# Reordering the prologue of an mLSTM cell with a SwiGLU FFN: 64-row turns, a GpSimd gate, late maxima behind the first products

## Chip, cores and metric

One core of one Trainium2 chip. The metric is the device time of one execution in microseconds (us), as the median of several runs. A profile of one execution shows where the time goes.

## The reference

The work is an mLSTM cell whose output feeds a feed-forward block. The cell runs over 768 tokens for 4 batches of 8 heads with 40 features. Its gates are stabilized with a running maximum:

```
m_new  = max(f[t] + m, i[t])
C      = exp(f[t] + m - m_new) * C + exp(i[t] - m_new) * v[t] k[t]^T
n      = exp(f[t] + m - m_new) * n + exp(i[t] - m_new) * k[t]
y[t]   = sigmoid(o[t]) * (C q[t]) / max(|n q[t]|, 1)
```

The rows y (3072 tokens by 320) go through `(silu(x @ w_gate) * (x @ w_val)) @ w_out` with a hidden width of 1536. The inputs of the cell are float32. The three weights are float64 and are turned into float32 on the chip, word by word.

## The kernel before

**Stages.** The tokens of all four batches are worked on in six groups of 128. The attention part of group 0 is the prologue; after it, the FFN of group g runs on TensorE while the other engines and short stretches of TensorE prepare group g+1. The FFN has twelve hidden blocks `hidden(g, m)` (gate and value products, silu on ScalarE, product on VectorE) and then the projection.

**Order.** The schedule is written out by hand: on each engine, instructions run in the order of the program. The lists `slots` and `ahead` say which pieces of other work are put behind or into block m of group 0. `first=` work of a block stands ahead of that block's silu and product, work of `slots[m]` behind them.

**Prologue (functions `first_*`).** Batches are handled in two pairs P of two batches u (heads 16P to 16P+15). W0 holds the decay weights of group 0, made by `first_mask`, `first_inputs`, `first_maxima` on TensorE and `first_exp` on ScalarE. `first_turn` turns k and q into feature rows with transposes of 128 x 128; `turn_one` does the same with transposes of 64 token rows, as the later groups do. `first_scores(P)` makes k-q products and VectorE multiplies them into W0. `first_own(u)` multiplies W0 with v; `first_x(u)` divides; `first_gate(P)` multiplies with the sigmoid of the output gate (`sig`) and copies the first 64 columns behind the last ones (GpSimd). `first_seam(P)` turns the rows into the FFN's input xT; `first_state` and `first_kept` make the state for group 1. `burn(n)` issues n idle products of 512 columns on TensorE.

**Maxima of the later groups.** `late_sums` scans the forget gates (VectorE) and subtracts (GpSimd); `late_maxima` is two small copies and a scan over 640 columns on 32 partitions; `late_decay` makes the decays; their exponential, `decay_rows`, `late_turns` (turn g and e, 10 transposes) and `decay` follow in the slots. The maxima go out to `M_dram`, and `weights_load(1)` reads them back into w_sb.

**Weights.** `piece_load(p)` loads piece p: gate columns into partitions 0 to 63 on SyncE's queue, value columns into partitions 64 to 127 on ScalarE's queue for p below 5. Piece 0 is block 0, piece 1 block 1, piece 2 blocks 2 and 3, piece 3 blocks 4 and 5. A converted block takes `scale(j)` (two ScalarE operations, L190 and L192), `join(j)` (two VectorE operations, L199 and L200) and `rounded(j)` (L207, on VectorE or on GpSimd, whose default it is). `top` has one buffer, so scale(j+1) waits for join(j). The `raw` tile has two buffers; pieces 2, 3 and 4 are loaded into parts of h_sb and wo_sb that are not in use yet, and piece 2's part holds W0 of batches 0 to 2, so that load waits for `first_own(2)`.

**PSUM.** Tiles come from two rings of four banks, "cell" and "gen". The FFN's products take "gen".

Of the kernel before, what the change touches and what calls it, by code (L numbers as in the profile page):

```python
# [12 lines left out]
U32 = mybir.dt.uint32  # L13
AF = mybir.ActivationFunctionType
ALU = mybir.AluOpType
# [9 lines left out]
def kernel(  # L25
# [47 lines left out]
    def flat(t):  # L73
        return t.rearrange("p c t -> p (c t)")

    def bank(name, tag="cell"):
        return psum.tile([128, 512], F32, name=name, tag=tag)
# [41 lines left out]
    def copy(eng, dst, src):  # L119
        if eng is nc.scalar:  # L120
            nc.scalar.copy(dst, src)
        else:
            eng.tensor_copy(dst, src)
# [58 lines left out]
                for c in range(0, n, 2):  # L182
                    blocks[NFC + (m + c) // 2] = (lo[:, c:c + 2], hi[:, c:c + 2], wo_sb[:, m + c:m + c + 2, :])

    def scale(j):
        if j in blocks:
            lo, hi, dst = blocks[j]
            a, d = hi.shape[1], hi.shape[2]
            top = conv.tile([128, NKC * 128], F32, name="top", bufs=1).rearrange("p (a d) -> p a d", a=a)
            nc.scalar.mul(top, hi.bitcast(F32), 2.0 ** -112)  # L190
            low = conv.tile([128, NKC * 128], I32, name="low").rearrange("p (a d) -> p a d", a=a)
            nc.scalar.mul(low, lo, 2.0 ** -29)  # L192
            blocks[j] = (low, top.bitcast(U32), dst)

    def join(j):
        if j in blocks:
# [81 lines left out]
    def late_maxima():  # L278
        nc.vector.tensor_copy(step1[:, 0:1, 0:1], f0[0:BH, end].unsqueeze(1))
        nc.vector.tensor_copy(step1[:, 1:, 0:1], f_sb[:, 0:NL - 1, last])  # L280
        nc.vector.tensor_tensor_scan(flat(M_sb), flat(step1), flat(i_sb), M0[0:BH, end], op0=ALU.add, op1=ALU.max)
# [6 lines left out]
    M_dram = tc.dram_tile([BH, S - L], F32, name="M_dram")  # L288


    def turn_one(P, src, dst, engs):
        tp = [bank("tp_kq").rearrange("p (a t) -> p a t", t=SUB) for _ in range(2)]
        for a in range(UA):
            h = P * UH + 2 * a
            for i in range(2):
                nc.tensor.transpose(tp[i][:, a, :], src[half(i), h:h + 2, :].rearrange("p h d -> p (h d)"),  # L296
                                    ident[half(i), half(i)])
        for i in range(2):
            copy(engs[i], dst[:, P * UA:(P + 1) * UA, half(i)], tp[i])
# [128 lines left out]
    def xT(n):  # L428
        return xTs[max(n - 1, 0) % 2]
# [36 lines left out]
    def burn(n, tag="cell"):  # L466
        t = bank("burn", tag)
        for _ in range(n):
            nc.tensor.matmul(t, lhsT=junk[:, 0:128], rhs=junk, start=True, stop=True)  # L469
# [2 lines left out]
        return slice(u * BH, (u + 1) * BH)  # L472

    A, V, G = nc.scalar, nc.vector, nc.gpsimd
    HH = H // 2
    wps = {}

# [21 lines left out]
    def first_values(P):  # L499
        nc.gpsimd.tensor_copy(w_end[:, heads(P)], W0[:, heads(P), end])  # L500
        nc.gpsimd.tensor_tensor(vw_sb[:, heads(P)], v_sb[:, heads(P)], w_end[:, heads(P)].to_broadcast([128, UH, D1]),
                                op=ALU.mult)

    def first_turn(P, src, dst, engs):
        for b in range(2):
            tp = bank("tp_kq").rearrange("p (a t) -> p a t", t=L)
            for a in range(UA // 2):
                h = P * UH + b * H + 2 * a
                nc.tensor.transpose(tp[:, a, :], src[:, h:h + 2, :].rearrange("p h d -> p (h d)"), ident)  # L509
            a = P * UA + b * UA // 2  # L510
            copy(engs[b], dst[:, a:a + UA // 2, :], tp)

    def first_scores(P):
        for b in range(2):
            sp = [bank("sp").rearrange("p (a t) -> p a t", t=L) for _ in range(2)]
            a0 = P * UA + b * UA // 2
            for a in range(UA // 2):
                for two in range(2):
                    nc.tensor.matmul(sp[two][:, a, :], lhsT=kT[half(two), a0 + a, :], rhs=qT[half(two), a0 + a, :],  # L519
                                     start=True, stop=True)  # L520
            W = W0[:, 2 * a0:2 * a0 + H].rearrange("p (a two) t -> p two a t", two=2)
            for two in range(2):
                nc.vector.tensor_tensor(W[:, two], sp[two], W[:, two], op=ALU.mult)
# [3 lines left out]
    def first_own(u):  # L527
        first_y[u] = bank("first_y", "gen")[:, 0:H * D1].rearrange("p (h d) -> p h d", d=D1)
        for h in range(H):
            nc.tensor.matmul(first_y[u][:, h, :], lhsT=W0[:, u * H + h, :], rhs=v_sb[:, u * H + h, :], start=True, stop=True)  # L530
# [7 lines left out]
        nc.vector.tensor_tensor(x_sb[:, u, 0:DM].rearrange("p (h d) -> p h d", d=D), y[:, :, 0:D],  # L538
                                den.to_broadcast([128, H, D]), op=ALU.mult)

    def first_gate(P):
        for u in (2 * P, 2 * P + 1):
            x = x_sb[:, u, 0:DM].rearrange("p (h d) -> p h d", d=D)
            nc.vector.tensor_tensor(x, x, o_sb[:, u * H:(u + 1) * H], op=ALU.mult)
        nc.gpsimd.tensor_copy(x_sb[:, 2 * P:2 * P + 2, DM:], x_sb[:, 2 * P:2 * P + 2, 0:HP])

    def first_state(P, tag="cell"):
# [7 lines left out]
    def first_kept(P, ps, eng):  # L555
        copy(eng, state(2)[:, P * UA:(P + 1) * UA], ps)

    def first_seam(P, engs):
        for c, eng in zip(range(0, NKC, 2), engs):
            cs = range(c, min(c + 2, NKC))  # L560
            tp = bank("tp_x")[:, 0:len(cs) * 2 * L].rearrange("p (c u s) -> p c u s", u=2, s=L)
            for w in cs:
                for b in range(2):
                    nc.tensor.transpose(tp[:, w - c, b, :], x_sb[:, 2 * P + b, ds(PAIRS[w][0] * HP, 2 * HP)], ident)
            copy(eng, xT(0)[:, c:c + len(cs), 2 * P * L:(2 * P + 2) * L].rearrange("p c (u s) -> p c u s", u=2), tp)

    burn(7)
    banks = [(u, j) for j in range(2) for u in range(B)]
# [6 lines left out]
    first_exp(1)  # L575
    first_values(0)
    first_scores(0)
    first_own(0)
    late_sums()
    first_turn(1, k_sb, kT, (A, A))  # L580
    first_x(0)
    first_turn(1, q_sb, qT, (A, V))
    load(o_sb, o_gate, 0, 1)
    piece_load(0)
    piece_load(1)
    late_maxima()
    first_own(1)
    first_values(1)
    first_scores(1)
    first_x(1)  # L590
    sig(0)
    burn(3)
    first_own(2)
    piece_load(2, h_sb[:, 1:1 + NKC])
    sig(1)
    burn(2)
    first_own(3)
    first_gate(0)
    first_x(2)
    first_x(3)  # L600
    first_gate(1)
    first_seam(0, (A, A, V))
    scale(0)
    ps1 = first_state(1, "gen")
    burn(1, "gen")
    piece_load(3, h_sb[:, NH - NKC:])
    join(0)
    first_seam(1, (A, A, V))
    rounded(0, V)
    first_kept(0, first_state(0), A)  # L610
    first_kept(1, ps1, V)
    late_decay()
    convert(1, V)
    nc.scalar.activation(warm, warm, AF.Silu)
    piece_load(4, wo_sb)
    piece_load(5)
    nc.sync.dma_start(out=M_dram, in_=flat(M_sb))


    pair = early.tile([BH, PP], F32)  # L620
# [102 lines left out]
    def load_all(dst, a, n):  # L723
        for P in range(2):
            load(dst, a, n, P)

    run = lambda f, *a: (lambda: f(*a))


    on_vector = (9, 10, 11)  # L730
# [1 line left out]
    ahead[0] = []  # L732
    ahead.update({4: [6], 5: [7, 8], 6: [9], 7: [10], 8: [11], 9: [], 10: [], 11: []})
    slots = {
        0: [run(convert, 2, V), run(load_all, k_sb, k, 1), run(load_all, q_sb, q, 1)],
        1: [run(piece_load, 6), run(nc.scalar.activation, step1, step1, AF.Exp), run(decay_rows)],
        2: [run(late_turns), run(weights_load, 1), run(load_all, v_sb, v, 1)],
        3: [run(decay)],
        5: [run(turn, 0, (A, A), (A, V))],
        6: [run(turn, 1, (A, A), (A, V)), run(piece_load, 7)],  # L740
        7: [run(weights_sub, 1, 0), run(weights_mask, 0), run(weights_sub, 1, 1), run(weights_mask, 1), run(nc.gpsimd.memset, q_sb, 0.0)],
# [112 lines left out]
```

## Time and profile before

| | |
|---|---|
| median of 3 runs | 552.01 us (551.99 to 552.12) |
| the profiled execution | 551.91 us |
| its span, first to last instruction | 549.9 us |
| busy: TensorE, VectorE, ScalarE, GpSimd | 544.7, 235.7, 135.8, 104.1 us |
| first product of the FFN starts | 31.91 us |
| last product ends | 546.8 us |
| granted TensorE clock | 1.000 |

Times in the views count from the first instruction of the span. A chain row is start, duration, engine, tile written and line of the kernel. In a timeline row, the bracket tells how long the engine was idle before it and what ended the wait. TensorE matmul ends are modelled. A row of a waits view tells who waited for whom, the total, how often, and the longest. A row of a stretch gives its limits and length, then the busy time of TensorE, its weight loads, VectorE, ScalarE and GpSimd, the granted clock, the DMA share, and GB/s.

### The profile page before, as it was taken

How to read it: one execution, taken by the hardware profiler on the slowest of the kernel's cores; microseconds unless marked ns; L12 is line 12 of the kernel's file. 1: busy time of each engine (PE TensorE's matmuls, PEld its weight loads, DVE VectorE, ACT ScalarE, POOL GpSimd, SP SyncE). 2: the span in 40 equal slices, each digit the busy share in tenths (PEclk: the TensorE clock that was granted, in tenths of full speed). 3: DMA queues.
4: the chain of work that ended last, by engine and by line, in shares of the span. 5: the costliest groups of instructions: out<-in, count | busy, mean ns of one | idle time of the engine just before them, and what ended most of it. 6: DMA issues, size and time to landing. Idle time of an engine off the chain costs nothing.

```text
span 549.9 us, 11590 instructions
## 1 busy us (share of the span) xinstructions
PE 544.7 (99%) x4987; PEld 311.6 (57%) x4989; DVE 235.7 (43%) x397; ACT 135.8 (25%) x203; POOL 104.1 (19%) x95
## 2 busy tenths in 40 slices
PE   8999999999999999999999999999999999999997
PEld 4964556774555575545575545576455567444475
DVE  5985769971346232455421545431436621111100
ACT  3376755252110133011024101115110100111100
POOL 2304265673011060011142011114001100000000
PEclk9999999999999999999999999999999999999999
DMA  9999997997431862660654551395000231000000
GB/s 126 183 287 181 193 268 157 149 108 113 52 50 26 129 109 55 74 73 12 102 104 100 64 71 14 58 145 115 1 1 2 35 63 37 12 1 0 2 24 24
DMA packets 223994, 45.69 MB, mean 83 GB/s; under 512 B 214504, under 2 KB 219112, under 8 KB 223944
## 3 DMA queue, kind: packets, MB, share of 16 engines
q1 hardware_dynamic: 222036, 42.11, 47.3%
q10 hardware_dynamic: 1908, 2.85, 2.1%
q8 instruction: 39, 0.64, 0.5%
q14 instruction: 11, 0.09, 0.1%
HBM read 35.68 MB, written 4.01 MB: 72 GB/s over the span
## 4 chain that ended last, share of the span: by engine, by line
PE 98%; DVE 1%; ACT 0%; issue 0%; ACTq 0%; DVEq 0%
PE gv_ps L654 57%; PE o_ps L670 24%; PE o_ps L677 5%; PE inter L377 2%; PE sp L331 2%; PE intra L382 2%; PE add L353 1%; PE first_y L530 1%; PE burn L469 1%; PE tp_kq L509 1%; PE sp L519 1%; PE wps L480 0%; PE tp_kq L296 0%; PE wps L484 0%; PE wps L489 0%; PE tp_x L439 0%
## 5 line engine op out<-in xcount | busy, mean ns | idle before, releaser
L654 PE MATMUL gv_ps<-xT,wgv_sb 64*128 64x512 f32 x1440 | 316.5, 593 | 0.3 <-DVE wgv_sb L207 0.3
L654 PEld LDWEIGHTS gv_ps<-xT,wgv_sb 64*128 64x128 f32 x1440 | 137.9, 187 | 159.2 <-issue 157.3
L660 DVE TENSOR_TENSOR h_sb<-sg,gv_ps 128x512 f32<-128x512 f32 x72 | 49.5, 688 | 216.9 <-ACT sg L659 216.9
L670 PE MATMUL o_ps<-wo_sb,h_sb 128*128 128x320 f32 x480 | 130.5, 434 | 0.0
L670 PEld LDWEIGHTS o_ps<-wo_sb,h_sb 128*128 128x128 f32 x480 | 90.8, 190 | 40.9 <-issue 3.8
L659 ACT ACTIVATE sg<-gv_ps 128x512 f32<-128x512 f32 x72 | 43.0, 597 | 266.3 <-PE gv_ps L654 266.1
L456 POOL TENSOR_SCALAR_AFFINE_SELECT w_sb<-w_sb 64x1024 f32<-64x1024 f32 x20 | 28.4, 1422 | 62.5 <-DVE w_sb L451 61.5
L362 POOL TENSOR_TENSOR C<-C,dec 128x328 f32<-128x328 f32 x20 | 14.5, 736 | 135.7 <-DVE C L369 135.7
L664 ACT COPY z_sb<-o_ps 128x320 f32<-128x320 f32 x24 | 10.0, 422 | 94.1 <-PE o_ps L670 90.6
L403 POOL TENSOR_TENSOR o_sb<-o_sb,y_sb 128x640 f32<-128x640 f32 x10 | 14.2, 1426 | 79.1 <-DVE y_sb L394 79.1
L677 PE MATMUL o_ps<-wo_sb,h_sb 128*128 128x320 f32 x96 | 26.9, 437 | 0.0
L451 DVE TENSOR_TENSOR w_sb<-g_T,w_sb 128x1024 f32<-128x1024 f32 x10 | 13.1, 1356 | 27.7 <-DMA w_sb<-M_dram 27.7
L426 DVE STREAM_TRANSPOSE xT<-x_sq 128x640 f32<-128x640 f32 x16 | 12.5, 822 | 22.4 <-DMA x_sq<-x_sb 22.4
L677 PEld LDWEIGHTS o_ps<-wo_sb,h_sb 128*128 128x128 f32 x96 | 17.9, 190 | 7.2
L394 DVE TENSOR_TENSOR y_sb<-y_sb,intra 64x328 f32<-64x328 f32 x40 | 19.7, 492 | 0.7
L369 DVE TENSOR_TENSOR C<-C,add 40x328 f32<-40x328 f32 (+1 forms) x36 | 17.7, 493 | 1.2 <-POOL C L362 0.6
L377 PEld LDWEIGHTS inter<-C,qT 64*64 64x64 f32 x640 | 10.2, 134 | 7.3 <-issue 6.1
L207 POOL TENSOR_TENSOR wgv_sb<-wgv_sb,low 128x640 int32<-128x640 int32 x6 | 9.2, 1539 | 24.0 <-DVE wgv_sb L200 24.0
L460 ACT ACTIVATE w_sb<-w_sb 128x1024 f32<-128x1024 f32 x10 | 10.6, 1058 | 11.8 <-POOL w_sb L456 11.7
L341 POOL TENSOR_TENSOR vw_sb<-v_sb,w_sb 128x656 f32<-128x656 f32 x10 | 12.8, 1303 | 0.4
L338 DVE TENSOR_TENSOR w_sb<-sp,w_sb 128x512 f32<-128x512 f32 x20 | 12.7, 682 | 0.0
L397 DVE TENSOR_SCALAR den<-den 128x16 f32<-128x16 f32 x10 | 12.1, 1214 | 0.3
(132 smaller groups left out, 345.3 us busy)
## 6 DMA issues: line engine op xcount, KB each, us to landing
w_sb<-M_dram SPq DMA_DIRECT2D x10, 512.0 KB, 8.7
x_sq<-x_sb SPq DMA_DIRECT2D x128, 40.0 KB, 2.0
k_sb<-in_k_dram SPq DMA_DIRECT2D x12, 320.0 KB, 6.0
v_sb<-in_v_dram SPq DMA_DIRECT2D x12, 320.0 KB, 5.8
o_sb<-in_o_gate_dram SPq DMA_DIRECT2D x12, 320.0 KB, 5.4
raw<-in_moe_w_out_dram SPq DMA_DIRECT2D x3, 1280.0 KB, 8.2
out_dram<-z_sb SPq DMA_DIRECT2D x24, 160.0 KB, 1.8
q_sb<-in_q_dram SPq DMA_DIRECT2D x32, 64.0 KB, 2.3
```

The lines of the kernel that those rows point to most:

```text
L362: nc.gpsimd.tensor_tensor(state(s + 1)[:, a], state(s)[:, a], dec[:, s - 2, a].unsqueeze(2).to_broadcast([128, UA, D1]), op=ALU.mult)
L369: nc.vector.tensor_tensor(c, c, ps[r], op=ALU.add)
L377: nc.tensor.matmul(inter[two][half(i), a, :], lhsT=qT[half(two), P * UA + a, half(i)], rhs=state(2 * n + i)[half(two), P * UA + a, :], sta ...
L394: nc.vector.tensor_tensor(t, t, intra[i][half(c)], op=ALU.add)
L403: eng.tensor_tensor(o, o, y[:, :, 0:D], op=ALU.mult)
L451: nc.vector.tensor_tensor(w_sb[:, heads(P)], gb, w_sb[:, heads(P)], op=ALU.subtract)
L456: nc.gpsimd.affine_select(w, w, compare_op=ALU.is_ge, fill=NEG, base=0, pattern=[[0, UH], [1, SUB]], channel_multiplier=-1)
L654: nc.tensor.matmul(ps[i], lhsT=wgv_sb[half(i), m, PAIRS[kc][i] if g < 2 else kc, :], rhs=x[half(i), kc, :], start=(kc == 0), stop=(kc == N ...
L659: nc.scalar.activation(sg, ps[0], AF.Silu)
L660: nc.vector.tensor_tensor(hid(g, m), sg, ps[1], op=ALU.mult)
L670: nc.tensor.matmul(p, lhsT=hid(g, m)[:, ts(u, L)], rhs=wo_sb[:, m, :], start=(m == 0), stop=(m == NFC - 1))
L677: nc.tensor.matmul(ps[u], lhsT=hid(g, m)[:, ts(u, L)], rhs=wo_sb[:, m, :], start=(m == 0), stop=(m == NFC - 1))
```

## The change

In the prologue, k and q of pair 1 are turned with `turn_one` (64-row transposes), k's into "gen" banks and ahead of `first_own(0)`. `first_gate(0)` runs on GpSimd. `first_x(1)` stands ahead of `first_scores(1)`; piece 1 is loaded behind `sig(0)`; three of the burns are gone. `scale` is split, and its first half stands between the first and the second copy of `first_seam(0)`; `rounded(0)` stands ahead of `first_seam(1)`. `late_maxima` moves into slot 0 of group 0, `late_decay` into slot 1, the store to `M_dram` behind the first k loads in slot 0; the exponential and `decay_rows` move to slot 2, `late_turns` to slot 3, `decay` to slot 4.

```diff
-    def scale(j):
+    def scale_top(j):
         if j in blocks:
             lo, hi, dst = blocks[j]
...
             nc.scalar.mul(top, hi.bitcast(F32), 2.0 ** -112)
+            blocks[j] = (lo, top.bitcast(U32), dst)
+
+    def scale_low(j):
+        if j in blocks:
+            lo, top, dst = blocks[j]
...
             nc.scalar.mul(low, lo, 2.0 ** -29)
-            blocks[j] = (low, top.bitcast(U32), dst)
+            blocks[j] = (low, top, dst)
+
+    def scale(j):
+        scale_top(j)
+        scale_low(j)
...
-    def turn_one(P, src, dst, engs):
-        tp = [bank("tp_kq").rearrange("p (a t) -> p a t", t=SUB) for _ in range(2)]
+    def turn_one(P, src, dst, engs, tag="cell"):
+        tp = [bank("tp_kq", tag).rearrange("p (a t) -> p a t", t=SUB) for _ in range(2)]
...
-    def first_gate(P):
+    def first_gate(P, eng):
...
-            nc.vector.tensor_tensor(x, x, o_sb[:, u * H:(u + 1) * H], op=ALU.mult)
+            eng.tensor_tensor(x, x, o_sb[:, u * H:(u + 1) * H], op=ALU.mult)
...
-    def first_seam(P, engs):
+    def first_seam(P, engs, between=None):
...
             copy(eng, xT(0)[:, c:c + len(cs), 2 * P * L:(2 * P + 2) * L].rearrange("p c (u s) -> p c u s", u=2), tp)
+            if between and c == 0:
+                between()
...
     first_scores(0)
+    turn_one(1, k_sb, kT, (A, A), "gen")
     first_own(0)
     late_sums()
-    first_turn(1, k_sb, kT, (A, A))
+    turn_one(1, q_sb, qT, (A, V))
     first_x(0)
-    first_turn(1, q_sb, qT, (A, V))
     load(o_sb, o_gate, 0, 1)
     piece_load(0)
-    piece_load(1)
-    late_maxima()
     first_own(1)
     first_values(1)
+    first_x(1)
     first_scores(1)
-    first_x(1)
     sig(0)
-    burn(3)
+    piece_load(1)
+    burn(2)
     first_own(2)
     piece_load(2, h_sb[:, 1:1 + NKC])
     sig(1)
-    burn(2)
     first_own(3)
-    first_gate(0)
+    first_gate(0, G)
     first_x(2)
     first_x(3)
-    first_gate(1)
-    first_seam(0, (A, A, V))
-    scale(0)
+    first_gate(1, V)
+    first_seam(0, (A, A, V), run(scale_top, 0))
+    scale_low(0)
     ps1 = first_state(1, "gen")
     burn(1, "gen")
     piece_load(3, h_sb[:, NH - NKC:])
     join(0)
+    rounded(0, V)
     first_seam(1, (A, A, V))
-    rounded(0, V)
     first_kept(0, first_state(0), A)
     first_kept(1, ps1, V)
-    late_decay()
     convert(1, V)
...
     piece_load(5)
-    nc.sync.dma_start(out=M_dram, in_=flat(M_sb))
...
-        0: [run(convert, 2, V), run(load_all, k_sb, k, 1), run(load_all, q_sb, q, 1)],
-        1: [run(piece_load, 6), run(nc.scalar.activation, step1, step1, AF.Exp), run(decay_rows)],
-        2: [run(late_turns), run(weights_load, 1), run(load_all, v_sb, v, 1)],
-        3: [run(decay)],
+        0: [run(convert, 2, V), run(late_maxima), run(load_all, k_sb, k, 1),
+            run(nc.sync.dma_start, out=M_dram, in_=flat(M_sb)), run(load_all, q_sb, q, 1)],
+        1: [run(piece_load, 6), run(late_decay)],
+        2: [run(nc.scalar.activation, step1, step1, AF.Exp), run(decay_rows), run(weights_load, 1), run(load_all, v_sb, v, 1)],
+        3: [run(late_turns)],
+        4: [run(decay)],
```

More of the change, by code (lines that the diff above doesn't have):

```diff
@@ L190, in scale @@
             nc.scalar.mul(top, hi.bitcast(F32), 2.0 ** -112)
+            blocks[j] = (lo, top.bitcast(U32), dst)
+    def scale_low(j):
+        if j in blocks:
+            lo, top, dst = blocks[j]
+            a, d = top.shape[1], top.shape[2]
             low = conv.tile([128, NKC * 128], I32, name="low").rearrange("p (a d) -> p a d", a=a)
             nc.scalar.mul(low, lo, 2.0 ** -29)
-            blocks[j] = (low, top.bitcast(U32), dst)
+            blocks[j] = (low, top, dst)
+    def scale(j):
+        scale_top(j)
+        scale_low(j)
     def join(j):
@@ L474 @@
     A, V, G = nc.scalar, nc.vector, nc.gpsimd
+    run = lambda f, *a, **b: (lambda: f(*a, **b))
     HH = H // 2
@@ L725, in load_all @@
             load(dst, a, n, P)
-    run = lambda f, *a: (lambda: f(*a))
     on_vector = (9, 10, 11)
```

## The prediction

> **What bounds the kernel now.** I read the page's chain that ended last first, then the chain in order of time, the engines' timeline from 0 to 60 us, the waits of SyncE's queue, and the busy time by stretches.
>
> ```profile
> PE 98%; DVE 1%; ACT 0%; issue 0%; ACTq 0%; DVEq 0%
> ```
>
> TensorE is the chain for 98% of the span. In order of time it holds work of another engine at two places only, both ahead of the first FFN product:
>
> ```profile
> 16.89 1.77 PE tp_kq L509 x16
> 18.66 1.71 PE first_y L530 x16
> 20.38 1.99 PE sp L519 x32
> ...
> 28.14 0.80 DVE x_sb L544 x2
> ...
> 30.95 0.83 DVE wgv_sb L207
> ...
> 31.91 13.15 PE gv_ps L654 x60
> 45.06 0.73 PE tp_g L628 x10
> ...
> 59.53 0.99 PE tp_kq L296 x32
> ```
>
> The columns are start, duration, what. From 31.91 on TensorE never waits noticeably until it ends at 546.8, so the time is "start of the first product" plus a fixed amount of TensorE work, unless a new wait appears. The change touches only what lies before 31.91 and the cover in blocks m = 0 to 4. Next, what stands behind the first blocks:
>
> ```profile
> 19.96 1.54 DVE L281 TENSOR_TENSOR_SCAN M_sb<-keep,M,i_sb 32x640 f32<-32x640 f32 x1
> ...
> 25.01 0.88 DVE L544 TENSOR_TENSOR x_sb<-x_sb,o_sb 128x320 f32<-128x320 f32 x2
> ...
> 28.18 0.60 SPq L165 DMA_DIRECT2D wo_sb<-in_moe_w_gate_dram  x1
> ```
> ```profile
> 40.17 0.20 PEld L654 LDWEIGHTS gv_ps<-xT,wgv_sb 64*128 64x128 f32 x2 [0.23 <-DVE wgv_sb L207]
> ...
> 41.58 1.54 POOL L207 TENSOR_TENSOR wgv_sb<-wgv_sb,low 128x640 int32<-128x640 int32 x1 [12.28 <-DVE wgv_sb L200]
> ```
> ```profile
> SPq L117 <- DMA h_sb<-in_moe_w_val_dram: 3.3, 1, 3.3
> SPq L165 <- DMA raw<-in_moe_w_gate_dram: 3.1, 2, 2.0
> ```
> ```profile
> 24.00:28.00 4.00, 4.00 (x36) 3.71 (x35) 3.61 (x15) 1.26 (x3) 0.29 (x1) 1.00 1.14 203
> ...
> 34.00:40.00 6.00, 6.00 (x30) 3.11 (x28) 3.96 (x6) 3.72 (x7) 0.00 (x0) 1.00 1.05 341
> ```
>
> VectorE is dense from 13.79 to 31.76 and holds the scan of late_maxima and gate(0). SyncE's issue at 28.18 was released by the landing of piece 0's gate half, so that half landed at about 28.17. SyncE then waited 3.3 us after the M_dram issue (33.17 + 0.36) for piece 2's value half: it landed at 36.85. The weight load of block 2 at 40.17 was released by L207 of block 2: that block has no cover at all today. The last two rows end in the DMA rate: 203 GB/s while one half of the partitions is written, 341 while gate and value halves are both in flight.
>
> **Profiled execution.** It took 551.91 us, a span of 549.9 and 2.0 around it; the median of the runs is 552.01, 0.1 more. I work in span times and carry the difference to the median.
>
> **The prologue after the change, TensorE.** The pair-1 k tile landed at 15.0 (issue 7.92 plus the shortest landing of that tile, 7.1). The turn now stands ahead of first_own(0), so TensorE waits about 0.5 us there (scores(0) ends at 14.5). A 64-row turn of 16 costs 0.50 (half of the L296 row, 0.99 for 32) against 0.89 (half of 1.77): two turns save 0.78. From 15.05: turn k 0.50, own(0) 1.71, turn q 0.50, own(1) 1.71, scores(1) 1.99, two burns 0.43, own(2) 1.71 plus 0.15 for the second half of its scaled scores, own(3) 1.71: 25.4. Then seam(0), state(1), burn, seam(1), state(0) at the distances of the present rows (1.22, 1.08, 0.1, 1.18, 1.13): 30.1. The pair-1 q tile is not seen to wait at 17.63 and is now wanted at 17.3: 0 to 0.3, I take 0. The k turn's "gen" banks were emptied by exponentials done by 13.5: no wait.
>
> **VectorE.** Own(1) ends at 19.5; first_x(1) 1.1; the four score products 2.48, ending at 23.2; first_x(2) follows own(2), first_x(3) follows own(3) and ends at 26.5; gate(1) 0.88, one xT copy 0.42: 27.8. Join 1.36 and rounding 0.95 end at 30.1, and the product follows in 0.15: 30.25. What leaves is 2.19 of late_maxima (19.31 to 21.50) and 0.88 of gate(0). TensorE and VectorE agree on 30.25, **1.66 earlier**.
>
> **GpSimd's gate.** L403 takes 1426 ns for 640 elements, so about 0.71 for each of the two 320-element products, plus the 0.29 copy. GpSimd is free at 22.6 (end of vw of pair 1) and sigmoid(0) ended at 21.7: done by 24.3, while seam(0) starts at 25.4. Beside a two-input VectorE scan, L501 took 2.53 instead of 1.29; with that factor it ends at 25.8, 0.4 late. Bounds 0 to 0.4; I take 0, because VectorE then runs products with one operand in PSUM, beside which L501 took 1.29.
>
> **Piece 0.** scale_top must start by 26.9 for the join at 27.8. Piece 1's value half (320 KB) is now issued behind sigmoid(0), some 2 us later, behind the gate half of piece 0. At 203 GB/s that takes 1.6 us from in front of it: 26.5. The other bound is 28.17, no change: then top, join, rounding give a start at 31.5, only 0.4 earlier. I take 26.8.
>
> **Three burns less** save 0.65, counted above. The first seven burns took 0.45 each, the last two 0.21; the granted clock reads 1.00 in all stretches. If the array fell back to the slow pace, up to 2 us of doubled work would follow. The longest gap I work out is 0.5 us; the trace shows gaps of 0.2 without a slowdown, so I take 0. The Trainium skill (TensorE: Matmul & The Clock Gate, Part 1) states an idle window of about 3.4 us before the clock halves; by that rule, too, the cost is 0, and no gap here tests it.
>
> **Blocks 0 to 3, what is given back.** Silu(0) moves from 36.48 to 34.82, and the scaling of block 2 from 36.97 to 35.31 if piece 2 has landed by 35.2. L207 of block 2 then ends at 38.46 (40.12 less 1.66). Now late_maxima stands behind it on VectorE: 2.19, to 40.65. Queued behind it are join(3) 1.36 (40.08 to 41.44 now), and GpSimd's rounding with its handoff, 1.68 (to 43.12): block 3 is ready at 43.7. TensorE asks for block 3 one block after block 2, at 40.17 + 4.28 = 44.45 in the old clock, 42.8 in the new one; the turn of the gates (0.73, L628), which gave block 3 cover before, has moved behind it. The wait is 0.9, of which a weight load hides some 0.1. **Balance: -1.66 + 0.86 = -0.8.** In general, against before: the larger of (gain of the start + 0.86) and (landing of piece 2 - 36.0).
>
> **Piece 2's landing.** Issued 1.2 us earlier (own(2) ends at 23.7 instead of 24.83), but the engines are busy throughout (DMA share above 1), so an earlier issue alone buys nothing. What could: gate and value halves would alternate earlier. Pieces 1 and 2 are 1920 KB: 9.5 us at 203 GB/s, 5.6 at 341, so 33.0 at best. Worst: 320 KB more in front, 1.6 later, 38.4. I take 35.2, nearest to the mixed row: value half 1 now falls between the gate halves. The skill (SBUF — State Buffer, "Can I just issue two DMAs to hit both halves?") says that transfers to the two halves serialize, +6%; by it piece 2 stays near 36.8 and the sum is +0.8. The row of 341 GB/s, with halves from two queues in flight, differs, and I go by the row.
>
> **The rest.** late_decay (1.07) stands behind product(1) ahead of join(4): 42.0 + 0.69 + 1.07 + 1.36 + 1.68 = 46.8, block 4 wanted at 43.7 + 4.28 + 0.73 = 48.7; 1.9 us of cover, and a blocked second input (up to 1.5 us, as L199 at 58.84, 1.14 for 0.49) still fits. M_dram passes two k loads on SP, which are being issued until 49.43; it then delays q, piece 6 and w_sb by 0.4. The q turn and the weight subtraction (71.47) start without a wait for them now: I take 0, at most 0.4. The exponential moves to slot 2 and the gates' turn to slot 3; E and g are used from slot 7 on: nothing.
>
> **Sum.** 552.0 - 0.8 = 551.2.
>
> **Rivals.**
> (1) *Block 3's wait is smaller.* If TensorE's weight loads or a shorter handoff hide more, up to the whole 1.66 stays: 550.4 to 550.9. For it: both engines agree on the start. Against: the order on VectorE is strict, and 2.19 us stand there.
> (2) *Slower: piece 2 lands as before or later, and late_maxima stands behind it.* The place is block 3's weights: ready at landing + 8.5. From 36.0 on the kernel loses; at 36.85 it loses 0.85 (552.9), at 38.4 it loses 2.4 (554.4). For it: saturated DMA engines, equal bytes in front. Against: the 341 GB/s row.
> (3) *Piece 0 still lands at 28.17.* The start gains 0.4, and block 3 takes it back: 552.4; between the bounds, 551.5 to 552.4. For it: the engines' backlog; against: 320 KB leave the front.
> That the change does not do what it says: a 64-row turn in "gen" waits for banks. Exponentials ended before; I give it nothing of its own.
>
> **Chances.** Forecast (-0.8 +-0.3) 0.37; rival 1 0.18; rival 3 0.17; rival 2 0.28, of it two thirds beyond 553.1. About 0.2% (1.1 us) is what a measurement here can tell from no change. Faster by more: rival 1 and a quarter of the forecast, 0.27; slower by more: 0.25, with the end of rival 3 and unseen waits; the rest, 0.48, within. The range 550.4 to 553.3 leaves out the late half of rival 2 and little else.
>
> **What would show it.** First gv_ps near 30.3; k turns of 0.5 us beginning at 15.0; L207 of block 2 followed at once by L279 to L281; a weight load of block 3 released by GpSimd's L207 some 0.9 late, and nothing late at block 4. Wrong if piece 2 lands after 36, if scale_top waits past 27, or if TensorE waits in any block after the third.

## The result, and the profile after

| | before | after |
|---|---|---|
| median on the first chip | 552.07 us (4 runs) | 556.16 us (554.9 to 556.25, 4 runs) |
| ratio, 95% interval | | 1.0061 [1.0042, 1.008] |
| the profiled execution, its span | 551.91, 549.9 us | 554.9, 552.4 us |
| first product of the FFN starts | 31.91 us | 34.05 us |
| mean granted TensorE clock | 1.000 | 0.994; 0.991 in two of the other runs |

The change made the kernel slower by 4.1 us; the forecast was 0.8 faster, and the range ended at 553.3. The first thing that differs on the page is the row of the clock, and then the chain of work that ended last:

```profile
PEclk9799999999999999999999999999999999999999
...
PE 90%; SPq 3%; DMA 2%; DVE 2%; POOL 1%; issue 1%; ACT 0%; ACTq 0%; POOLq 0%
```

The second slice (13.8 to 27.6 us) ran at 0.7 of the clock. In the chain in order of time the start looks like this (start, duration, what):

```profile
7.47 7.42 DMA k_sb<-in_k_dram
14.90 0.14 issue
15.03 0.71 PE tp_kq L306 x16
15.74 1.91 PE first_y L541 x16
17.65 0.83 PE tp_kq L306 x13
18.48 3.56 PE first_y L541 x16
22.05 3.29 PE sp L530 x32
...
25.88 3.50 PE first_y L541 x32
...
34.05 17.45 PE gv_ps L663 x80
51.50 0.73 PE tp_g L637 x10
```

The turn of k waits for its tile until 15.03, as forecast. But own(1) (18.48) takes 3.56 where own(0) took 1.91, and the scores 3.29 where the kernel before has 1.99. The view by stretches names the reason. Its rows end in the granted clock, the share of the DMA and GB/s; the first six figures behind the limits are the length and the busy time of TensorE, of its weight loads, of VectorE, of ScalarE and of GpSimd:

```profile
14.51:17.92 3.41, 2.89 (x42) 2.80 (x44) 2.54 (x3) 1.07 (x2) 0.81 (x2) 1.00 1.48 151
17.92:21.33 3.41, 3.41 (x28) 3.29 (x22) 1.63 (x5) 2.56 (x3) 2.74 (x3) 0.50 0.94 167
21.33:24.75 3.42, 3.42 (x30) 3.34 (x31) 1.62 (x5) 0.04 (x1) 2.01 (x3) 0.50 1.21 209
24.75:28.00 3.25, 3.25 (x34) 2.98 (x32) 2.31 (x6) 0.00 (x0) 0.00 (x0) 1.00 1.06 186
```

In the kernel before, the clock reads 1.00 throughout, here from 14 to 22 us:

```profile
14.00:18.00 4.00, 3.83 (x40) 3.55 (x37) 3.93 (x8) 1.06 (x3) 0.31 (x2) 1.00 1.32 140
18.00:22.00 4.00, 4.00 (x53) 3.95 (x52) 3.78 (x7) 2.98 (x4) 3.92 (x4) 1.00 1.17 204
```

In the changed kernel it was halved from 17.92 to 24.75, that is for two windows of 3.413 us. A window at half speed takes up to 1.7 us of work away. Two make a mean clock of 0.994, three 0.991, so two of the three runs at 556 lost three; the third (556.22) lost two, like the profiled one. The only idle time of TensorE in the neighbourhood is the wait for k (view of waits, last figure the longest):

```profile
PE tp_kq L306 <- DMA k_sb<-in_k_dram: 1.1, 1, 1.1
```

The steps that concern the blocks, in the timeline (in brackets the idle time before):

```profile
21.45 0.86 POOL L555 TENSOR_TENSOR x_sb<-x_sb,o_sb 128x320 f32<-128x320 f32 x1 [0.70 <-ACT o_sb L473]
```
```profile
42.30 0.21 PEld L663 LDWEIGHTS gv_ps<-xT,wgv_sb 64*128 64x128 f32 x2 [0.22 <-DVE wgv_sb L217]
46.94 0.30 PEld L663 LDWEIGHTS gv_ps<-xT,wgv_sb 64*128 64x128 f32 x4 [0.57 <-POOL wgv_sb L217]
```

The weight load of block 3 does wait for GpSimd's rounding, as forecast. The products don't: in the chain above, the 80 products of blocks 0 to 3 run through in 17.45 us, at the 0.22 us each of the kernel before's 60 in 13.15. The loads of a block otherwise start some 0.4 us ahead of its products (block 2: load at 42.30, product at 42.71), and that lead took up the wait.

From the first weight load of block 0 to that of block 9 it takes 42.03 us before and 42.03 after, so the blocks give back nothing. Of the 2.5 us by which the span is longer, 2.14 lie in the start. The other 0.4 lie behind block 9 and come and go from run to run: from the first product to the end of the span it takes 518.0 and 517.6 us in the two traces of the kernel before, 518.4 here and 517.7 in a second trace of the same kernel (e17 below). Outside the span the profiled execution spends 2.5 us; the kernel before spends 2.0.

### The profile page after: what moved, and what is told of

It reads as the page before. It is cut to its first block, busy times and chain, and to the rows that moved or that the text cites. A ratio compares the mean times of both kernels' runs of the same rounds, so it can differ in the third digit from the quotient of the medians.

```text
span 552.4 us, 11621 instructions
## 1 busy us (share of the span) xinstructions
PE 546.7 (99%) x5002; PEld 315.0 (57%) x5002; DVE 235.4 (43%) x395; ACT 136.0 (25%) x203; POOL 104.6 (19%) x97
## 4 chain that ended last, share of the span: by engine, by line
PE 90%; SPq 3%; DMA 2%; DVE 2%; POOL 1%; issue 1%; ACT 0%; ACTq 0%; POOLq 0%
PE gv_ps L663 56%; PE o_ps L679 24%; PE sp L341 2%; PE inter L387 2%; PE first_y L541 2%; PE intra L392 2%; PE add L363 1%; DMA k_sb<-in_k_dram 1%; SPq L325 1%; SPq L117 1%; DMA out_dram<-z_sb 1%; DVE y_sb L404 1%; PE tp_kq L306 1%; PE sp L530 1%; POOL wo_sb L217 1%
## 5 line engine op out<-in xcount | busy, mean ns | idle before, releaser
L663 PEld LDWEIGHTS gv_ps<-xT,wgv_sb 64*128 64x128 f32 x1440 | 139.5, 187 | 158.2 <-issue 154.4
L436 DVE STREAM_TRANSPOSE xT<-x_sq 128x640 f32<-128x640 f32 x16 | 12.5, 822 | 22.5 <-DMA x_sq<-x_sb 22.5
L473 ACT ACTIVATE o_sb<-o_sb 128x640 f32<-128x640 f32 x12 | 8.7, 735 | 15.5 <-DMA o_sb<-in_o_gate_dram 8.4
```

What stands on the lines that cost most here:

```text
L663: nc.tensor.matmul(ps[i], lhsT=wgv_sb[half(i), m, PAIRS[kc][i] if g < 2 else kc, :], rhs=x[half(i), kc, :], start=(kc == 0), stop=(kc == N ...
```

## The experiments

Several chips served, and each kernel is compared with runs of the kernel before on its own chip. The kernel before itself lost the clock in 5 of 35 runs on one of them and in none of 90 on the four others, so the share of runs below 0.998 of the clock is given with each time: it, not the median, is what most of these runs are about.

### The wait, the thin turns, the fillers

**e1**: the changed kernel with the k turn where it waits for nothing.

```diff
-    turn_one(1, k_sb, kT, (A, A), "gen")
     first_own(0)
+    turn_one(1, k_sb, kT, (A, A), "gen")
```

> The changed kernel with one move: the k turn of pair 1 stands behind first_own(0) again. Theory 'wait': in the changed kernel TensorE stands idle for 1.06 us (13.97 to 15.03) until pair 1's k has landed, the granted clock falls to one half from 17.92 for 6.83 us, and that is the loss. Then here the clock stays at 1.00, the first gv_ps starts at 30.3 to 30.7 instead of 34.05, and the time is 551.0 to 551.6. Theory 'thin work': the 64-row turns and the three missing burns keep the array too little busy, whatever the wait. Then the clock falls here too and the time stays at 554 to 556.

552.55 us, ratio 0.9983 [0.9956, 1.0011]; 4 of 12 runs lost clock, on the chip on which 5 of 35 runs of the kernel before did. The loss from 18 to 25 us is gone, but the profiled run lost one window at another place:

```profile
22.74:26.16 3.42, 3.42 (x33) 3.42 (x32) 2.27 (x7) 0.74 (x1) 1.17 (x3) 1.00 1.21 203
26.16:29.57 3.41, 3.41 (x32) 3.08 (x31) 2.66 (x9) 2.15 (x4) 0.29 (x1) 0.50 1.12 196
```

This row speaks against a theory of idle gaps: in the window before the loss the profile, which models the ends of matmuls, has TensorE busy for 3.42 of 3.42 us. It held little but own(2) and own(3), whose matmuls of 41 columns follow each other every 111 ns while the weight loads are busy throughout (the second 3.42); a filler passes 512 columns in 215 ns.

**e2**: the changed kernel with five fillers (the idle products of `burn`) in the wait.

```diff
+    burn(5, "gen")
     turn_one(1, k_sb, kT, (A, A), "gen")
     first_own(0)
```

> The changed kernel with five burns (512 columns each, some 0.21 us) ahead of the k turn of pair 1, so that TensorE works while it waits for the tile; the order stays as changed. Theory 'wait': clock at 1.00, first gv_ps at 30.2 to 30.7, 551.0 to 551.5. A theory that the order itself costs (GpSimd's gate, late_maxima ahead of block 3) gives 552.5 to 554 even with a full clock. Theory 'thin work' expects the burns to help as well, so this run does not tell it from 'wait'.

552.57 us, ratio 1.0011 [0.9978, 1.0043]; 8 of 12 runs kept the clock (551.7 to 552.8), 4 did not (557.1 to 557.8). All four runs of the changed kernel on the first chip had lost clock, so filling the wait seems to help, but does not settle it.

**e3**: the kernel before with its wide (128-row) k turn ahead of own(0), so that it waits there as in the changed kernel. **e4**: the kernel before with the thin turns of 64 rows, in place.

```diff
 e3:
+    first_turn(1, k_sb, kT, (A, A), "gen")
     first_own(0)
     late_sums()
-    first_turn(1, k_sb, kT, (A, A))
 e4:
-    first_turn(1, k_sb, kT, (A, A))
+    turn_one(1, k_sb, kT, (A, A))
...
-    first_turn(1, q_sb, qT, (A, V))
+    turn_one(1, q_sb, qT, (A, V))
```

> The kernel before with one move: the 128-row k turn of pair 1, into gen banks, stands ahead of first_own(0), so TensorE waits for that tile; all burns and all else as before. Theory 'wait': TensorE idles 0.5 to 1.1 us there, the clock falls to one half for one or two stretches of 3.4 us, and the time is 554 to 556. Theory 'thin work': nothing thin was added, the clock stays, and the time is 552.0 to 552.6.

> The kernel before with pair 1's k and q turned on tiles of 64 rows at their old places, and nothing else. Theory 'wait': clock at 1.00, and 551.7 to 552.2, since VectorE is dense up to the first product and TensorE's 0.78 us saved find little to move. Theory 'thin work': the clock falls in the stretch of the turns, 554 to 556.

552.88, ratio 0.9987 [0.9963, 1.0011], and 552.45, ratio 0.9983 [0.9961, 1.0006]; no run of 12 lost clock in either, so neither the wait alone (0.8 us in e3's trace) nor the thin turns alone did it.

From here on the theory was that a window is judged by its *array work*. I counted, in the trace, the columns of all matmuls in a window times their rows over 128, in fillers (512 columns, 128 rows, 0.215 us at full pace; a window could hold 16).

**e5**: the changed kernel again. **e6**: the changed kernel with fillers everywhere (five in the wait; three and two ahead of own(2) and own(3) as before). **e7**: only the old three and two put back. **e8**: the kernel before with three fillers less.

```diff
 e6, e7:                         e8 (kernel before):
-    burn(2)                     -    burn(3)
+    burn(3)                     +    burn(2)
     first_own(2)                     first_own(2)
...
+    burn(2)                     -    burn(2)
     first_own(3)                     first_own(3)
```

> The changed kernel unaltered, on one chip with the other three. Theory A (the clock goes where a stretch of 3.41 us holds too little array work, counted as matmul columns times rows over 128): in the changed kernel every 3.41 us stretch between 13.5 and 21 us holds under 0.2 of the array's full work whatever the phase, so every run loses the clock, 0.991 to 0.994, 555 to 556.5 us. Theory B (the four runs on the first chip were a chance of that chip, as the kernel before also has single runs of 555 to 558): most runs keep the clock, about 552.3.

> The changed kernel with five filler matmuls ahead of the k turn (in the wait for the k tile) and with the kernel before's three and two fillers ahead of own(2) and own(3). Theory A (sparse stretch): both empty stretches are filled, the lowest stretch is 0.18 at 16.5 (nearly kept in the run with fillers in the wait alone) and about 0.3 at 23.5, so at most one run in ten loses the clock; the time is that of the fillers-in-the-wait kernel at full clock plus up to 0.65 for the three fillers: 552.2 to 553.0. Theory C (another cause: the order or GpSimd's gate makes the loss at 23 to 26, not the missing fillers): a third of the runs still at 557.

> The changed kernel with only the kernel before's three and two fillers ahead of own(2) and own(3) put back; the wait ahead of the k turn and the turns on 64 rows stay. Theory A (sparse stretch): the stretch from 13.5 to 18 stays at 0.13 to 0.2 in every phase, so most runs (8 of 12 or more) still lose the clock at 14 to 18 and take 554.5 to 557; once the clock is lost there the later fillers don't win it back. Theory D (the three fillers removed are the whole cause): none loses, 552.0 to 552.8.

> The kernel before with three of its fillers less and nothing else: two ahead of own(2), none ahead of own(3). Theory A (sparse stretch): the stretch from 22.5 to 24 sinks from 0.26 to 0.1 to 0.17, as in the changed kernel with fillers in the wait, so about a third of the runs (2 to 7 of 12) lose the clock and take 554 to 558; the others gain up to 0.6: 551.5 to 552.3. Theory E (the loss needs the wait or the thin turns as well): none loses, all at 551.3 to 552.7.

| kernel | lost clock | median | ratio | runs at full clock |
|---|---|---|---|---|
| e5 | 9 of 12 | 555.65 | 1.0041 [1.0021, 1.0062] | 552.2 to 552.8 |
| e6 | 2 of 12 | 552.67 | 1.0014 [0.9999, 1.0029] | 551.9 to 553.2 |
| e7 | 7 of 10 | 555.13 | 1.0043 [1.0021, 1.0065] | 552.2 to 552.9 |
| e8 | 7 of 12 | 552.62 | 1.0009 [0.9995, 1.0023] | 551.5 to 552.4 |
| before | 0 of 33 | 552.16 | | |

e5 says that the loss belongs to the changed kernel (not every run, as was expected, but three of four). e8 is the cleanest edit: three fillers less, 0.6 us of idle products, and more than half of the runs lose a window, where none of 33 did with them; the five that lose none are 0.45 faster than the kernel before by their median. The fillers keep the clock up; that they save time on the whole isn't shown, as the interval includes 1. e7 loses with the old fillers back, and e6, with the wait filled as well, loses far less, so the wait is one cause of its own. That it takes the thin turns besides fits e3 and e4, but isn't shown: e7 holds all other moves of the change too, and no run has the wait and the thin turns alone. In e7's profile:

```profile
14.26:17.67 3.41, 2.37 (x34) 2.31 (x32) 3.09 (x4) 1.07 (x2) 0.26 (x1) 1.00 1.43 142
17.67:21.08 3.41, 3.41 (x29) 3.21 (x28) 1.62 (x5) 1.80 (x2) 3.30 (x4) 0.50 1.14 181
21.08:24.50 3.42, 3.42 (x26) 3.34 (x27) 1.03 (x4) 0.81 (x2) 1.43 (x2) 0.50 1.16 209
24.50:27.91 3.41, 3.41 (x24) 2.55 (x22) 2.58 (x4) 0.00 (x0) 0.58 (x2) 0.50 1.05 186
```

Once halved, the same instructions fill the next windows even less (own(1) takes 3.6 us), and the clock stays down until a window holds more. That fits the counts: by the mean clock, e5's nine runs that lost clock lost one to four windows (one run six), e8's seven about one each.

### Where the shorter start goes at full clock

**e9**: e1 with the old fillers back, as in e6. **e10**: e6 with the later maxima behind the join of block 3, and what follows them a slot later. **e11**: both. **e12**: e11 with piece 3 issued later.

```diff
 e10, e11, e12:
-        0: [run(convert, 2, V), run(late_maxima), run(load_all, k_sb, k, 1),
-            run(nc.sync.dma_start, out=M_dram, in_=flat(M_sb)), run(load_all, q_sb, q, 1)],
-        1: [run(piece_load, 6), run(late_decay)],
-        2: [run(nc.scalar.activation, step1, step1, AF.Exp), run(decay_rows), run(weights_load, 1), ...],
-        3: [run(late_turns)],
-        4: [run(decay)],
+        0: [run(convert, 2, V), run(load_all, k_sb, k, 1), run(load_all, q_sb, q, 1)],
+        1: [run(piece_load, 6), run(late_maxima), run(nc.sync.dma_start, out=M_dram, in_=flat(M_sb))],
+        2: [run(late_decay), run(nc.scalar.activation, step1, step1, AF.Exp), run(weights_load, 1), ...],
+        3: [run(decay_rows)],
+        4: [run(late_turns)],
+        5: [run(decay), run(turn, 0, (A, A), (A, V))],
 e12:
-    piece_load(3, h_sb[:, NH - NKC:])
...
+    piece_load(3, h_sb[:, NH - NKC:])
     convert(1, V)
```

> The changed kernel with its k turn behind own(0), where it waits for nothing, and with the kernel before's three and two fillers put back: no sparse stretch under 0.2, so the clock stays at 1.0 in nearly all runs, and gv starts at 31.0 to 31.4, 0.5 to 0.9 ahead of the kernel before. Theory F (floor): the weights of block 2 are ready 3.3 us after the landing of piece 2 (36.8 to 37.2), so block 2 still starts at 40.2 to 40.4 and block 3 at 44.9 to 45.1; the span ends within 0.2 of the kernel before's 549.9 and the time within 0.3 of 552.2. Theory S (the start carries through): block 2 starts 0.5 to 0.9 earlier than with all fillers (40.33), and the time falls by that, to 551.3 to 551.7.

> The kernel with all fillers (wait, own(2), own(3)), and the later maxima moved one slot on, behind the join of block 3; the later decay, its rows, the gate turns and the decay product each one slot on as well. Theory G (block 3's join waits behind the maxima): GpSimd rounds block 3 by 43.2 instead of 44.92, block 3 starts at 44.3 instead of 44.97, the end comes 0.6 earlier: 552.0 to 552.2 beside 552.7 with the maxima in front. Rival: the 1.8 us of the maxima now delay block 4's or block 5's join, and what is won at block 3 is lost there: 552.5 to 552.9.

> Both edits: the k turn behind own(0) with the old fillers, and the maxima behind the join of block 3. Theory F (floor by the landing of piece 2): block 2 at 40.2 to 40.4 as in the others, block 3 at 44.2 to 44.4, so the same time as with the fillers in the wait and the maxima moved: 552.0 to 552.2. Theory S: another 0.5 to 0.9 off, 551.3 to 551.6.

> As the one with both edits, and the load of piece 3 is issued some 3 us later (ahead of the conversion of block 1, at about 31.5 instead of 28.3), so that piece 2 has the engines of the DMA to itself for that long. Theory F (floor by the landing of piece 2): piece 2 lands 1 to 2.5 us earlier (34.5 to 36.0), block 2 starts at 39.4 to 39.7, gv block 6 at 59.4 to 59.8 instead of 60.3 to 60.5, the time is 551.2 to 551.6. If the landing is no floor: nothing changes against the one with both edits. Rival on the other side: piece 3 lands 2 to 3 us later (42.5 to 43.5), and block 4 (top at 43.3 to 44) comes late by up to 0.5.

In this section the start of a block, and so of "the first product", is its first weight load, if nothing else is said.

e9: 552.06 us, ratio 1.0 [0.9991, 1.0009], no loss of clock in 11 runs. From the first scores to the first product it takes 18.65 us instead of 19.35, and from there to block 9 42.06 instead of 42.03. Yet the median is that of the kernel before.

The lists of runs answer a part of that. The median span of e9 is 549.6 us, that of the kernel before 550.0 on the same chip: 0.4 of the 0.7 is there. But the time less the span is 2.40 to 2.51 us in every run of e9 and 1.87 to 2.16 in the kernel before's, so what was won inside the span is lost outside of it. This holds in all runs: 2.39 to 2.53 for the changed kernel and the experiments made from it, 1.85 to 2.28 for the kernel before and e3, e4, e8 and e14, which are made from it. Which move of the change lengthens this stretch isn't shown; a wide turn in the wait (e3), thin turns (e4), fewer fillers (e8) and later maxima (e14) don't, each alone in the kernel before.

Block 2 starts 8.28 behind the first product, as in the kernel before (8.29), so the floor by piece 2 did not bind in this trace. It binds in e2, where ScalarE waits for the value half, and block 2 starts 8.57 behind the first product, which delays the products of block 3 by 0.23:

```profile
37.20 0.79 ACT L190 ACTIVATE top<-h_sb 128x640 f32<-128x640 f32 x1 [0.19 <-DMA h_sb<-in_moe_w_val_dram]
```

e10, e11 and e12 are slower: 556.47, 555.16 and 557.38, ratios 1.0094 [1.0075, 1.0113], 1.0063 [1.0042, 1.0083] and 1.0107 [1.0078, 1.0135]; 14 of their 18 runs lost clock, e10's profiled one at 63.7, behind the wait that follows. Block 3 starts 12.56 behind the first product in e11 instead of 12.93, but there was nothing to win: its products start 12.95 us behind the first one in e9 and in e11 alike. And my own order made a new wait, the turn of q behind VectorE's copy of the decay product (the columns are those of the timeline):

```profile
59.03 0.71 PE L306 MATMUL tp_kq<-ident,k_sb 64*128 64x64 f32 x16
...
61.75 0.71 PE L306 MATMUL tp_kq<-ident,q_sb 64*128 64x64 f32 x15 [1.95 <-DVE dec L653]
```

In e12 the value half of piece 2 landed at 37.4, not earlier (36.6 in e9 and e11): the later issue of piece 3's value half did nothing for it in this trace, and block 2 came 8.99 behind the first product.

**e13**: e11 with the exponential in slot 3, `decay_rows` behind the gates' turn in slot 4, and `decay` in slot 7. **e14**: the kernel before with these slots, the maxima and the decay taken out of its prologue.

```diff
-        2: [run(late_decay), run(nc.scalar.activation, step1, step1, AF.Exp), run(weights_load, 1), ...],
-        3: [run(decay_rows)],
-        4: [run(late_turns)],
-        5: [run(decay), run(turn, 0, (A, A), (A, V))],
+        2: [run(late_decay), run(weights_load, 1), ...],
+        3: [run(nc.scalar.activation, step1, step1, AF.Exp)],
+        4: [run(late_turns), run(decay_rows)],
+        5: [run(turn, 0, (A, A), (A, V))],
...
+        7: [run(decay), ...],
```

> The kernel with the k turn behind own(0) and the old fillers, the later maxima behind the join of block 3, the exponential one slot later, so that it finds its input done, the gate turns in slot 4 and the decay product in slot 7, behind both turns: the kernel with both edits lost 1.95 us where the turn of q waited for VectorE's copy of the decay product, and 1.67 us of ScalarE at the exponential. Theory G (block 3's join waits behind the maxima): block 3 starts 12.5 instead of 12.93 us behind the first gv product, block 6 28.45 minus 0.5 to 0.9, and the time is 551.2 to 551.6 where the kernel before takes 552.07. Rival (the maxima are paid wherever VectorE does them, since its joins hand over the weights one by one): block 6 at 28.3 to 28.6 again and 551.9 to 552.3.

> The kernel before with its start as it was, fillers and all, except that the later maxima and the decay leave the prologue for the same slots (1, 2, 3, 4, 7). Theory T (the maxima cover nothing and cost nothing in the prologue, TensorE sets the start; what pays is the order of blocks 3 to 6): gv starts where it did, the clock stays at 1.0, and the time falls by 0.2 to 0.6 as the gate turns no longer stand ahead of block 3: 551.4 to 551.9. Theory V (VectorE's 3.9 us in the prologue are on the path of the start): the first gv product comes 0.5 to 1.6 us earlier and the time falls by 0.6 or more, if piece 2's landing allows it.

554.11 us, ratio 1.0043 [1.0021, 1.0064], and 553.98, ratio 1.0033 [1.0012, 1.0053]. In e13 the weight load of block 3 no longer waits (4.27 us from block 2 to block 3 instead of 4.65; the products again come 12.95 behind the first), and block 6 starts 27.75 behind the first product instead of 28.45; by block 9 the difference is gone (42.03), since the decay product now stands ahead of block 8 (4.97 instead of 3.98). By block 12 it is 1.4 behind e9. So both theories missed: block 6 came as early as theory G says, but the time is above even the rival's. That what the maxima cost is paid wherever VectorE does them is not shown. In e14 the second half of o landed at 28.0 (25.0 in the kernel before) and the gate half of piece 0 at 29.8 (28.2), the first product came at 33.19, and both theories missed again. Why the transfers came later in this trace isn't shown; the runs that kept the clock, 554.0 in the median, say that here the maxima did not leave the prologue for nothing.

**e15**: e1 again. **e16**: e1 with `burn(1)` ahead of own(3). **e17**: the changed kernel, **e18**: the kernel before, each once more for a trace.

> The changed kernel with its k turn behind own(0) once more, for a trace in which the clock stays at 1.0 (two of three runs). From the first scores to the first gv product then 18.2 to 18.4 us, 1.0 to 1.15 less than in the kernel before (19.35). Theory F (floor by the landing of piece 2): block 2 starts 3.3 us behind the landing of piece 2's value half (36.6 to 37.4), so at 40.0 to 40.7, more than 8.3 us behind the first gv product, and the gain is gone by block 3. Theory S (it carries through): block 2 starts 8.28 behind the first gv product and the gain is still there at block 12.

> The changed kernel with its k turn behind own(0) and one filler ahead of own(3), two ahead of own(2). Sparse stretch: the stretch at 22.5 to 24.5 rises from 0.15 by 0.06 to 0.21, so at most one run in twelve loses the clock, where with none of it four of twelve did. Theory F: the time is still that of the kernel before within 0.3 (552.0 to 552.4 if that takes 552.1). Theory S: 0.4 to 0.8 less.

> The changed kernel once more, for its trace: sparse from 13.5 to 21 us, so the clock is lost again in three of four runs, in windows of 3.41 us whose number (1 to 4) depends on where the windows fall; the windows before each loss hold under 0.19 of the array's work.

> The kernel before once more, for a second trace of it. From the first scores to the first gv product 19.3 to 19.4 us as in its first trace (19.35), since nothing waits for a transfer there that varies; the first scores themselves start between 12.4 and 13.3, as they do in the traces of the other kernels (12.15 to 13.33), so that the start differs by up to 0.6 from run to run whatever the order behind it. If instead the first scores start at 12.5 again, the later first scores of the kernels with the k turn behind own(0) (13.1 in three of five traces) belong to them, and explain why a start that is 0.7 to 1.1 us shorter is not seen in their times.

e15 and e17 lost one window each (553.43 and 553.05 us) and so don't show the kernel at full clock. e15's loss follows the same stretch as e1's (a window from 22.84 on, TensorE busy for 3.41 of 3.41 us), on a chip on which none of 17 runs of the kernel before lost clock. e16: 552.92 us, ratio 1.0018 [1.0, 1.0035], with 4 of 12 runs short of clock, where one was expected; its profiled run kept the clock:

```profile
15.72 1.75 PE first_y L541 x14
17.48 1.14 PE tp_kq L306 x32
18.62 1.91 PE first_y L541 x16
20.52 1.99 PE sp L530 x32
22.51 0.54 PE burn L479 x2
23.05 1.76 PE first_y L541 x16
24.82 0.21 PE burn L479
25.03 1.71 PE first_y L541 x16
...
31.42 17.45 PE gv_ps L664 x80
48.88 0.73 PE tp_g L638 x10
```

Here 18.28 us lie between the first scores and the first product, 1.07 less than before, 42.04 from there to block 9, and the execution took 551.51. So the shorter start does carry through in this trace (theory S); block 2 started at 39.67, 8.28 behind the first product and 3.3 behind the landing of piece 2 (36.4), which is just at the floor. The other runs at full clock took 551.8 to 553.2, where the kernel before took 552.3 in the median. e18 gives 19.35 again from the first scores to the first product, but its first scores began at 12.97 instead of 12.53; e16's at 13.11. That begin differs by a good half microsecond from run to run. Of e9's 0.7 us, 0.4 is lost outside the span; the rest stays open, and the interval of e9 reaches to 0.5. No version beat the kernel before clear of noise; e9 equals it.

## Why the prediction was wrong

**The step that failed is "Three burns less": "I take 0" for the clock, with up to 2 us if the array fell back.** The clock did fall back, for two or three windows in the four runs of the result, and the 3.41 us of work that two of them take are more than the bound. The reasoning was by the longest gap (0.5 us). The measured wait was 1.06, the first scores having begun early in that run, but a gap was the wrong quantity: e1 lost the clock behind a window without any. I did add up the fillers' 0.65 us as a gain, and read the kernel before's clock of 1.00 in every stretch as a state that needs no upkeep. e8 shows that the fillers kept it up. Nor did I put the three edits together: the wait takes work out of the stretch from 13.5 to 18, the 64-row turns give half of the rows there, and the missing fillers empty 22.5 to 25.

**The rule of the Trainium skill** that I cited (TensorE: Matmul & The Clock Gate, Part 1, an idle window of about 3.4 us) gave cost 0 as well. The length of the window agrees with the runs (3.413 us), "idle" does not: the windows before the seven losses between 8 and 35 us that the traces show had TensorE busy for 2.4 to 3.4 us of it, as the profile counts busy time.

**The start.** The wait for k ended at 15.03, as forecast (15.05). The terms behind it were too small: a thin turn took 0.64 instead of 0.50 (e2, e17), and the own() behind it 1.91 instead of 1.71, so 0.68 us of the 1.66 were never there. Less the 3.41 us of two half windows, the changed kernel's first product would have come at 30.6, and with the 15.85 us that e2 took from its k turn to the first product at 30.9 (both estimates); forecast was 30.25.

**GpSimd's gate** took 0.86 instead of 0.71 and ended, copy included, at 24.5, before it was wanted. **Piece 0**'s gate half landed at 26.0 (forecast: between 26.5 and 28.17, 26.8 taken), so rival 3 falls.

**Blocks 0 to 3.** This is the second term that was off: +0.86 was forecast, and it measured 0. The weight load of block 3 is late by some 0.37 (4.64 behind block 2's, 4.27 in e13, where it doesn't wait). But its products start 12.95 us behind the first product in both: a block's loads lead its products by some 0.4 us, and I had let them hide 0.1. The gates' turn and the decay product cost the same in their new places: block 6's products start 28.44 behind the first one before and 28.45 after. For this block rival 1's mechanism, the weight loads hiding the wait, was the right one.

**Piece 2** landed at 36.4 to 37.4 in the traces at full clock, not 35.2; that was rival 2's landing. But the weight load of block 2 was late by 0.3 in e2, where the start was early for its piece, and by 0.7 in e12, whose piece landed at 37.4; in the others it was not, and rival 2's 0.85 did not come. **Rival 2 named the right sign with a mechanism that had no part in it**: none of my cases held the clock as a mechanism of the slower side.

At full clock the forecast gain is not seen either: the changed kernel's own runs at full clock took 552.2 to 552.8, the kernel before 552.16 on that chip. A part of this is a term that the prediction held fixed: it put "2.0 around" the span, and in every run of the changed kernel this is 2.4 to 2.5. What takes back the rest of the shorter start wasn't found.

## What to carry to other kernels

Before taking out filler products, adding a wait or making matmuls thinner near the start, count the array work in every stretch of 3.4 us, columns times rows, not the busy share: a TensorE that reads 100% busy can still be sparse. Judge edits that thin the same stretch together: the wait and the thin turns each passed alone here, and the changed kernel with the old fillers back did not. Before repairing a late weight load, look whether the products behind it are late as well. Compare spans as well as times, since a change can move what passes outside the span. And run a kernel near the edge a dozen times with the granted clock of each run beside its time: medians of 552.6 hid losses in a third (e1, e2) and in more than half (e8) of the runs.

## What the hardware showed

This is the count on which the theory of array work rests, over all traces between 8 and 35 us, in windows of 3.413 us laid from the start of the full clock, in fillers out of 16:

| window | array work | TensorE busy | next window |
|---|---|---|---|
| e7, 14.26 | 2.3 | 2.37 of 3.41 us | half |
| e1, 22.74 | 2.4 | 3.42 of 3.42 | half |
| e17, 16.95 | 2.8 | 3.42 of 3.42 | half |
| changed kernel, 14.51 | 2.9 | 2.89 of 3.41 | half |
| e2, 16.27 | 3.1 | 3.41 of 3.41 | full |
| e8, 24.24 | 3.2 | 3.42 of 3.42 | full |

Seven losses there followed windows of 2.3 to 2.9 fillers; every window that kept the clock held 3.05 or more. At half clock, windows with 2.7 or less stayed at half, and 3.4 or more brought the full clock back. Columns alone don't sort them: e8's window holds 3.2 fillers by columns and keeps the clock, the changed kernel's holds 4.5 and loses it; with the rows counted they are 3.2 and 2.9. Later in the kernels one window of 2.9 (e10, at 60.3) lost, and one of 2.2 (e11, at 57.7) did not, so the count is no law; some matmul records can be missing.

Nor does it rank the kernels. Runs of the same kernel differ in what they lose, which fits windows whose phase against the program changes from run to run (in the three traces of the changed kernel windows begin at 14.10, 14.51 and 16.95), but the phase was not set by any experiment. If every phase were equally likely, e4 should lose in a good quarter of its runs: a window laid at 14.3 in its trace would hold 2.3, and windows below 3.0 fit in 0.9 of the 3.4 us of phases, yet none of 12 runs lost clock. e6 has 1.4 us of such phases and lost in 2 of 12 runs, e8 0.7 us and lost in 7 of 12. So sparse array work is what all early losses in the traces followed; what else decides is open. e16 shows the margin: its lowest stretch, wherever the window is laid, holds 3.0, and a third of its runs lost clock.
